# Windowed attention and FFN on one core: scores of a head pair on 64 rows each, values on 64 columns each, from float16 products

## The chip, the core and the metric

The kernel runs on one core of a Trainium2 chip. The core has a matrix engine (TensorE, PE in the profile; its weight loads are PEld), a vector engine (VectorE, DVE), an activation engine (ScalarE, ACT), a general engine (GpSimd, POOL) and a queue engine (SyncE, SP) that here issues DMA transfers. Each engine works through its own instructions in order; semaphores tie them together. The metric is device time in microseconds (us) of one execution, the median of several.

## The reference

Attention over 8 sequences of 576 positions with 8 heads of 64, each query seeing its own and the 127 positions before, with a bias that falls with distance (a slope of 2^-(head + 1)). Its output, 4608 rows of 512, goes through a feed-forward layer of width 2048.

```python
scores = scale * np.matmul(q, k.transpose(0, 1, 3, 2))
mask = (rel >= 0) & (rel < window)
scores = np.where(mask, scores + bias[None], -1000000000.0)
attn = np.exp(scores - np.max(scores, axis=-1, keepdims=True))
attn = attn / (np.sum(attn, axis=-1, keepdims=True) + 1e-09)
x = np.matmul(attn, v)
h = x @ w_in
g = np.where(h >= 1, h, np.where(h <= -1, 0.0, (h + 1) ** 2 / 4))
return g @ w_out
```

All of it is float32. The kernel keeps float32 accuracy with cheaper products: an operand is split into a high part and the rest, and products of the parts are summed.

## The kernel before

The 4608 rows are 12 chunks of 384 (three query blocks of 128). Per chunk, attention works through 4 head pairs (p, 48 in all), two heads m = 2p, 2p + 1 each; the FFN follows in 16 blocks of 128 columns (fc). Layer 1 of a block (L508 to L510) is 12 float16 matmuls of 384 columns, layer 2 (L539 to L541) 9 of 512, two blocks behind. While the FFN of chunk c runs, the attention of chunk c + 1 is emitted between its steps. Chunks 0 and 1 (LIGHT = 2) take plain float32 products in attention; chunk 0 also converts the float64 weights.

From chunk 2 on, a pair goes through these steps:

- q and k are loaded with both heads one above the other: 64 rows of head 0, 64 of head 1. `prepare_q` and `prepare_k` round them to a shorter float (qp, kp) and keep the rest, on ScalarE and VectorE. DMAs then copy the parts into ql (per head: q rounded on its 64 rows, q's rest on the other 64) and kk, kl (k rounded and k's rest, each on both halves): 12 copies per pair on SP's queue. With them two matmuls per block cover all products of the parts on 128 rows (L404, L405).
- `scores` takes one head: three blocks, two of them in a first PSUM bank, one in a second. VectorE adds the bias and takes the row minimum of the negated scores (L408), ScalarE takes the exponential with its sum (L410), VectorE normalises into ep (L416 to L421).
- `weights_t` transposes ep (L429), ScalarE and VectorE split it into float16 parts lu (L441, L442), GpSimd masks them (L444, L446).
- v is loaded (`load_v`, L294), its largest value found (`reach_of_v`, L302, VectorE), turned into a scale for the whole chunk (`scale_x`), and split into float16 parts vs (`prepare_v`, L373, L374).
- `values` takes one head: 8 matmuls (6 where no earlier block exists) whose 128 output rows hold the product with v's high part on 64 and with its rest on the other 64 (L483). ScalarE copies one half (L485), VectorE adds the other (L486) into xn.
- At the FFN's first step of a chunk, `split_x` makes the float16 parts xh and xl of xn (L501, L502), which layer 1 reads.

The order is written as a list, `segments`, one short function per entry, and a chunk's FFN step emits its share of the next chunk's entries. A scheduler then orders each engine's instructions by its own estimate of when each could start. Buffers that matter: the attention's PSUM pool has 3 banks, layer 1 has 2, vn has 6 tiles, z and ep 1, lu 2.

## Time and profile before

| | us |
|---|---|
| median of 3 runs (1077.75 to 1080.46) | 1077.77 |
| the profiled execution | 1081.46 |
| its span, first to last instruction | 1079.8 |
| TensorE busy in it | 995.4 (92%) |
| VectorE busy | 779.5 (72%) |
| ScalarE busy | 623.5 (58%) |
| GpSimd busy | 383.0 (35%) |

The mean granted TensorE clock of the profiled execution is 0.954 of full speed. A record of a matmul ends later than the next one starts, since matmuls are pipelined: a rate is read from starts. Row groups give the line in the program, the engine, the operation, output and inputs by name, the shape, the count, then busy time and the mean of one in ns, then the idle time of the engine just before them with what ended it.

### The profile page before, as it was taken

What the parts mean: (1) busy time and instruction counts of PE and PEld (TensorE: products, weight loads), DVE (VectorE), ACT (ScalarE), POOL (GpSimd) and SP (SyncE); (2) the same over time, 40 slices, a digit from 0 to 9 for tenths busy, and PEclk for the clock granted to TensorE, in tenths of its full rate; (3) what the DMA queues carried; (4) which work ended last, traced back from release to release, by engine and by line L of the source; (5) the groups of instructions that cost most, each with busy time, mean ns of one, the idle gap of its engine ahead of it and who ended that gap; (6) DMA issues with size and microseconds to landing.
All of it is one profiled execution on the core that took longest, in us unless ns stands there. A gap on an engine that the chain in (4) does not pass through costs nothing.

```text
span 1079.8 us, 17781 instructions
## 1 busy us (share of the span) xinstructions
PE 995.4 (92%) x5682; PEld 601.5 (56%) x5682; DVE 779.5 (72%) x2115; ACT 623.5 (58%) x1467; POOL 383.0 (35%) x461
## 2 busy tenths in 40 slices
...
GB/s 231 111 149 217 176 81 113 81 102 100 112 77 141 121 80 130 130 86 100 99 108 75 155 119 80 117 127 82 117 96 106 120 73 109 133 71 54 30 1 30
DMA packets 91677, 114.42 MB, mean 106 GB/s; under 512 B 11200, under 2 KB 66496, under 8 KB 91584
## 3 DMA queue, kind: packets, MB, share of 16 engines
...
q8 instruction: 45, 0.74, 0.3%
q14 instruction: 48, 0.39, 0.1%
...
## 4 chain that ended last, share of the span: by engine, by line
PE 47%; DVE 23%; DMA 12%; ACT 7%; SPq 5%; issue 4%; POOL 1%; ACTq 0%; DVEq 0%; POOLq 0%
PE h L508 7%; PE h L509 7%; PE h L510 7%; PE acc L539 6%; PE acc L540 6%; PE acc L541 6%; DMA vn<-in_v_dram 4%; ACT z L410 4%; DMA qr<-in_q_dram 4%; DVE g L516 3%; DMA ql<-qr 3%; DVE g L517 3%; DVE z L408 2%; SPq L364 2%; PE x L483 2%
## 5 line engine op out<-in xcount | busy, mean ns | idle before, releaser
L525 POOL TENSOR_TENSOR gl<-g,gh 128x384 f16<-128x384 f32 x176 | 170.0, 967 | 410.5 <-ACT gh L524 399.3
L508 PE MATMUL h<-xh,wi 128*128 128x384 f16 x768 | 255.7, 335 | 14.8 <-DVE g L517 12.5
L509 PE MATMUL h<-xl,wi 128*128 128x384 f16 x768 | 258.0, 336 | 11.8 <-DVE xl L502 11.7
L510 PE MATMUL h<-xh,wi 128*128 128x384 f16 x768 | 257.7, 336 | 0.5 <-DVE i_in L158 0.5
L516 DVE SCALAR_TENSOR_TENSOR g<-u,half 128x384 f32<-128x384 f32 x176 | 120.7, 688 | 116.1 <-ACT u L515 110.5
L539 PE MATMUL acc<-wo,gh 128*128 128x512 f16 x528 | 201.1, 381 | 0.0
L540 PE MATMUL acc<-wo,gh 128*128 128x512 f16 x528 | 200.8, 380 | 0.0
L541 PE MATMUL acc<-wo,gl 128*128 128x512 f16 x528 | 198.2, 379 | 0.0
L524 ACT CAST gh<-g 128x384 f16<-128x384 f32 x176 | 89.2, 510 | 179.1 <-DVE g L517 152.7
L410 ACT ACTIVATE z<-z,nmax 128x256 f32<-128x256 f32 (+2 forms) x288 | 138.5, 482 | 69.9 <-DVE nmax L408 67.0
L515 ACT ACTIVATE u<-h,shift,fall 128x384 f32<-128x384 f32 x176 | 116.5, 665 | 64.2 <-PE h L510 63.3
L444 POOL TENSOR_SCALAR_AFFINE_SELECT lu<-lu 128x768 f16<-128x768 f16 x80 | 74.1, 926 | 127.8 <-DVE lu L442 116.7
L509 PEld LDWEIGHTS <-wi 128*128 128x128 f16 x768 | 76.8, 100 | 72.9 <-issue 21.3
L510 PEld LDWEIGHTS <-wi 128*128 128x128 f16 x768 | 76.9, 100 | 66.5 <-issue 20.6
L517 DVE SCALAR_TENSOR_TENSOR g<-h,gain,g 128x384 f32<-128x384 f32 x176 | 107.5, 614 | 3.8
L508 PEld LDWEIGHTS <-wi 128*128 128x128 f16 x768 | 76.8, 100 | 58.3 <-issue 7.1
L408 DVE CUSTOM_DVE_ANT_0 z<-s,rel 128x256 f32<-128x256 f32 (+2 forms) x256 | 93.9, 392 | 6.5 <-PE s L405 3.2
L404 PE MATMUL s<-kk,ql 128*128 128x256 f32 (+2 forms) x240 | 77.8, 347 | 4.8 <-DVE xn L486 4.8
L541 PEld LDWEIGHTS <-gl 128*128 128x128 f16 x528 | 51.5, 98 | 54.8
L446 POOL TENSOR_SCALAR_AFFINE_SELECT lu<-lu 128x768 f16<-128x768 f16 x80 | 79.2, 989 | 4.9
L483 PE MATMUL x<-lu,vs 128*128 128x256 f16 (+1 forms) x592 | 68.1, 260 | 12.4 <-POOL lu L446 9.9
L539 PEld LDWEIGHTS <-gh 128*128 128x128 f16 x528 | 52.0, 98 | 48.8 <-issue 1.4
...
## 6 DMA issues: line engine op xcount, KB each, us to landing
...
```

The source lines that it names most:

```text
L408: V.tensor_tensor_reduce(out=z[:, i, c0:], in0=o, in1=r[:, c0:], op0=ALU.add, op1=ALU.min, scale=-slope if c else -0.125, scalar=3.0e38, a ...
L410: S.activation(z[:, i, c0:], z[:, i, c0:], AF.Exp, bias=nmax[:, i:i + 1], scale=-1.0, accum_out=sm[:, i, 0:1])
L508: T.matmul(ph, wi[fc][:, 0, cc, :], xh, start=(cc == 0), stop=False)
L509: T.matmul(ph, wi[fc][:, 0, cc, :], xl, start=False, stop=False)
L510: T.matmul(ph, wi[fc][:, 1, cc, :], xh, start=False, stop=(cc == NCC - 1))
L515: first = S.activation(u, ph, AF.Relu, bias=shift[c] if c else quarter, scale=fall[c][:, col])
L516: V.scalar_tensor_tensor(g, u, half[c] if c else 0.5, u, ALU.min, ALU.mult)
L517: last = V.scalar_tensor_tensor(g, ph, gain[c][:, col] if c else fall[c][:, col], g, ALU.mult, ALU.max)
L525: G.tensor_tensor(gl, g, gh, ALU.subtract)
L539: T.matmul(a, gh[:, ts], wo[fc][:, 0], start=first, stop=False)
L540: T.matmul(a, gh[:, ts], wo[fc][:, 1], start=False, stop=False)
L541: T.matmul(a, gl[:, ts], wo[fc][:, 0], start=False, stop=last)
```

## The change

From chunk 2 on:

- q and k stay on their own rows, head 0 on rows 0 to 63 and head 1 on 64 to 127, and are split into float16 parts there (`split_qk`), scaled by the largest values of q per row and of k for the chunk. Those come from ScalarE (`reach_of`, absolute value into a scratch tile with an accumulated result), VectorE and one matmul of 256 columns (`level`, `scale_all`). The bias tables and slopes are rescaled per chunk.
- `scores_of_pair` computes both heads at once: per block three products (high x high, high x rest, rest x high) for each head, each on 64 rows of the array, the two heads alternating, each head with a PSUM bank of its own.
- `values_of_pair` computes both heads into one bank: each product on 64 columns of the array, heads alternating. xh and xl are taken from that bank directly; copy, sum and `split_x` go.
- the DMA copies of q and k go; `load_all` requests q, k and v of a pair five pairs ahead.
- z and ep get two tiles, lu three. The list of segments is rewritten, so that a chunk counts as ready with its last pair's values.

```diff
         st = pair.setdefault(p, {})
         qr = st["qr"] = ap1.tile([P, CH], F32, name=f"qr_{p}", tag="qr")
         DMA.dma_start(qr, q[g * P:(g + 1) * P, c * CH:(c + 1) * CH])
+        kr = st["kr"] = kz[p % 2]
+        for j, r in enumerate(lo_rows):
+            DMA.dma_start(kr[r, j, :n], k[g * P + j * D:g * P + (j + 1) * D, (c + 1) * CH - n:(c + 1) * CH])
...
+    def load_all(p):
+
+        c, g = divmod(p, NPAIR)
+        n = CH + before(c) * P
+        if c == LIGHT:
...
+        pair[p] = dict(q=t[:, :CH], k=t[:, CH:CH + n])
+        DMA.dma_start(pair[p]["q"], q[g * P:(g + 1) * P, c * CH:(c + 1) * CH])
+        DMA.dma_start(pair[p]["k"], k[g * P:(g + 1) * P, (c + 1) * CH - n:(c + 1) * CH])
+        load_v(p)
...
+    def reach_of(p):
+
+        reach_of_v(p)
+        for x in "qk":
+            f = pair[p][x]
+            S.activation(junk[:, :f.shape[1]], f, AF.Abs, accum_out=tops[c, x][:, g:g + 1])
...
+    def level(c):
...
+        V.tensor_scalar(iq.bitcast(I32), rq.bitcast(I32), 0x7F800000, None, ALU.bitwise_and)
...
+        V.tensor_tensor(t, rk, iq, ALU.mult)
+        V.tensor_reduce(top[:, 0:1], t, X, ALU.max)
+        V.tensor_reduce(top[:, 1:2], tops.pop(c)[:, :NPAIR], X, ALU.max)
...
+        for a in range(2):
+            G.tensor_scalar(d[:, a], ident, top[:, a:a + 1], None, ALU.mult)
...
+    def scale_all(c):
...
+        T.matmul(b, ones, diag.pop(c).rearrange("p a w -> p (a w)"), start=True, stop=True)
...
+        V.tensor_reduce(i_2[c], b.rearrange("p (a w) -> p a w", w=P), X, ALU.max)
...
+        V.tensor_scalar(s_k[c], tops.pop((c, "i")), s_2[c][:, 0:1], None, ALU.mult)
+        V.tensor_scalar(z_of[c], fade, i_2[c][:, 0:1], None, ALU.mult)
...
+        V.tensor_scalar(rels[c][0], rel, s_2[c][:, 0:1], -1.0e38, ALU.mult, ALU.max)
...
+    def split_qk(p):
...
+        t = pair[p]["h"] = ap1.tile([P, 2, 2 * CH + P], F16, name=f"h_{p}", tag=("kl", "kk")[p % 2])
+        for x, s1, a, b in (("q", s_q[c], 0, CH), ("k", s_k[c], CH, CH + n)):
+            f, s1 = pair[p].pop(x), s1[:, g:g + 1]
+            S.activation(t[:, 0, a:b], f, AF.Copy, scale=s1)
+            V.scalar_tensor_tensor(t[:, 1, a:b], f, s1, t[:, 0, a:b], ALU.mult, ALU.subtract)
...
-        qp = ap1.tile([P, CH], F32R, name=f"qp_{p}", tag="qp")
-        S.activation(qp, qr, AF.Copy, scale=scale)
-        V.scalar_tensor_tensor(qr.bitcast(F32R), qr, scale, qp.bitcast(F32), ALU.mult, ALU.subtract)
...
-        for j in range(2):
-            DMA.dma_start(ql[lo_rows[j], j].bitcast(F32), qp[lo_rows[j]].bitcast(F32))
-            DMA.dma_start(ql[hi_rows[j], j].bitcast(F32), qr[lo_rows[j]])
-
-    def prepare_k(p):
...
-        S.copy(kp[:, :n], kr[:, :n])
-        V.tensor_tensor(kr[:, :n].bitcast(F32R), kr[:, :n], kp[:, :n].bitcast(F32), ALU.subtract)
...
-        for t, f in ((kk, kp.bitcast(F32)), (kl, kr)):
-            for j in range(2):
-                for r in lo_rows:
-                    DMA.dma_start(t[r, j, :n].bitcast(F32), f[lo_rows[j], :n])
...
-        S.activation(vs[:, :n, :, 0, :], vn[:, :n], AF.Copy, scale=s_x[c])
-        V.scalar_tensor_tensor(vs[:, :n, :, 1, :].rearrange("p i j d -> p (i j) d"), vn[:, :n].rearrange("p i j d -> p (i j) d"),
...
+        f = pair[p].pop("vn")[:, :n].rearrange("p i j d -> p i (j d)")
+        vs = pair[p]["vs"] = wp.tile([P, 2, NQB + 1, P], F16, name=f"vs_{p}", tag="f_i", bufs=3)
+        S.activation(vs[:, 0, :n], f, AF.Copy, scale=s_x[c])
+        V.scalar_tensor_tensor(vs[:, 1, :n], f, s_x[c], vs[:, 0, :n], ALU.mult, ALU.subtract)
...
+    def scores_of_pair(p, blks):
...
+        pts = [bank(f"s_{2 * p + j}_{blks[0]}").rearrange("r (m w) -> r m w", w=2 * P) for j in range(2)]
+        last = []
+        for n, i in enumerate(blks):
+            c0, k0 = window(c, i)
+            for s, (a, b) in enumerate(((0, 0), (0, 1), (1, 0))):
+                for j, r in ((1, lo_rows[1]), (0, lo_rows[0])):
+                    behind(last, lambda: last.append(
+                        T.matmul(pts[j][:, n, c0:], t[r, a, i * P:(i + 1) * P], t[r, b, CH + k0:CH + k0 + 2 * P - c0],
+                                 start=(s == 0), stop=(s == 2)).ins))
+                    last = last[-1:]
+        for j in range(2):
+            soften(2 * p + j, blks, pts[j])
+
...
+            head[m] = dict(ep=ap1.tile([P, NQB, P], F32, name=f"ep_{m}", tag="ep", bufs=2),
...
+                           ap1.tile([P, NQB, 2 * P], F32, name=f"z_{m}", tag="z", bufs=2),
...
-            T.matmul(o, ql[:, j, i * P:(i + 1) * P], kk[:, j, k0:k0 + 2 * P - c0], start=True, stop=False)
-            T.matmul(o, ql[:, j, i * P:(i + 1) * P], kl[:, j, k0:k0 + 2 * P - c0], start=False, stop=True)
...
+            factor = -0.125 if c == 0 else -2.0 ** -(m % H + 1) if c < LIGHT else z_of[c][:, m % H:m % H + 1]
+            V.tensor_tensor_reduce(out=z[:, i, c0:], in0=pt[:, n, c0:], in1=r[:, c0:], op0=ALU.add, op1=ALU.min,
+                                   scale=factor, scalar=3.0e38, accum_out=nmax[:, i:i + 1])
...
+        lu = head[m]["lu"] = ap1.tile([P, 2, 2 * NQB, P], F16, name=f"lu_{m}", tag="lu", bufs=3)
...
-        todo = [(i, s) for i in [*range(NQB), -1] if i + b0 >= 0 for s in range(2)]
-        for n, (i, s) in enumerate(todo):
-            w = vs[:, i + b0, j].rearrange("p s d -> p (s d)")
...
-            T.matmul(px[:, q0 * P:q1 * P], w, lu[:, s, first:first + q1 - q0, :].rearrange("p a w -> p (a w)"),
-                     start=(n == 0), stop=(n == len(todo) - 1), skip_group_check=True)
-        S.copy(o, px[D:, :])
-        V.tensor_tensor(o, px[:D, :], o, ALU.add)
...
+    def values_of_pair(p):
...
+        vs = pair.pop(p)["vs"]
+        lus = [head.pop(2 * p + j)["lu"] for j in range(2)]
+        px = bank(f"x_{p}")[:, :CH]
+        todo = [(i, a, b) for i in [*range(NQB), -1] if i + b0 >= 0 for a, b in ((0, 0), (0, 1), (1, 0))]
+        last = []
+        for n, (i, a, b) in enumerate(todo):
+            q0, q1 = max(i, 0), min(i + 2, NQB)
+            first = 2 * i + 1 if i >= 0 else 0
+            for j, r in enumerate(lo_rows):
+                behind(last, lambda: last.append(
+                    T.matmul(px[r, q0 * P:q1 * P], vs[:, a, i + b0, r], lus[j][:, b, first:first + q1 - q0, :].rearrange("p a w -> p (a w)"),
+                             start=(n == 0), stop=(n == len(todo) - 1), skip_group_check=True).ins))
+                last = last[-1:]
...
+        S.activation(xh, px, AF.Copy, scale=1.0 / TOP)
+        V.scalar_tensor_tensor(xl, px, 1.0 / TOP, xh, ALU.mult, ALU.subtract)
+        xs.setdefault(c, []).append((xh, xl))
...
+    for p in range(M1 // 2, NP):
+        c, g = divmod(p, NPAIR)
...
+        if new:
+            segments.append([lambda p=p: reach_of(p + NPAIR)])
+        segments.append([lambda p=p: scores_of_pair(p, (0, 1))])
+        if new and g == NPAIR - 1:
+            segments.append([lambda c=c: level(c + 1)])
+        segments.append([lambda p=p: scores_of_pair(p, (2,))])
+        segments.append([lambda p=p: split_v(p)])
+        if p > M1 // 2:
+            segments.append([lambda p=p: values_of_pair(p - 1)])
+            if g == 0:
+                ready.append(len(segments))
+        if new and g == NPAIR - 1:
+            segments.append([lambda c=c: scale_all(c + 1)])
+        segments.append([lambda p=p: weights_t(2 * p)])
+        segments.append(([lambda p=p: split_qk(p + 1)] if p + 1 < NP else []) + ([lambda p=p: load_all(p + 5)] if p + 5 < NP else []))
+        segments.append([lambda p=p: weights_t(2 * p + 1)])
+    segments.append([lambda: values_of_pair(NP - 1)])
+    ready.append(len(segments))
```

How it moves instructions, at three places. On VectorE, the boundary between the FFNs of chunks 8 and 9, before: attention's last sum of chunk 9 (xn_9_3, L486) and the split that layer 1 of chunk 9 waits for (xl_9_3, L502) stand behind the maximum of a v tile (rows_11) and next to work of chunk 10; block 15 of chunk 8 lies 27 rows ahead of the first of these.

```order
L302 TENSOR_REDUCE rows_11_9907<-vn_46_10188 128x1
L486 TENSOR_TENSOR xn_9_3_9788<-x_79_9909,xn_9_3_9788 64x384
L374 SCALAR_TENSOR_TENSOR vs_41_10185<-vn_41_8899,s_x10_9870,vs_41_10185 128x8x64
L408 ISA z_81_9976,nmax_81_9977<-s_81_0_9978,rel_110 128x256
L408 ISA nmax_81_9977 128x1
L408 ISA z_81_9976,nmax_81_9977<-s_81_0_9978,rel_end_122 128x256
L408 ISA nmax_81_9977 128x1
L408 ISA z_81_9976,nmax_81_9977<-s_81_2_9996,rel_110 128x192
L408 ISA nmax_81_9977 128x1
L329 TENSOR_SCALAR o_g10_10981<-r10_10978 128x1
L502 SCALAR_TENSOR_TENSOR xl_9_3_10033<-xn_9_3_9788,xh_9_3_10032 128x384
```

The same place after the change: xl_9_3 stands ahead of block 15 of chunk 8 (g_8_15, L593 and L594 now), and eight small rows lie between that block and g_9_0.

```order
L567 SCALAR_TENSOR_TENSOR xl_9_3_9863<-x_39_9843,xh_9_3_9862 128x384
L485 RECIPROCAL rc_80_9805<-rc_80_9805 128x3
L425 SCALAR_TENSOR_TENSOR vs_42_10318<-vn_42_9187,s_210_9628,vs_42_10318 128x512
L485 RECIPROCAL rc_81_9813<-rc_81_9813 128x3
L593 SCALAR_TENSOR_TENSOR g_8_15_9898<-u_8_15_9897,half8_8923 128x384
L489 TENSOR_TENSOR ep_80_9771<-z_80_9772,rc_80_9805 128x384
L408 TENSOR_SCALAR shift10_10910<-u10_10906 128x1
L326 TENSOR_SCALAR i_q11_10523<-rows_q11_9731 128x4
L489 TENSOR_TENSOR ep_81_9778<-z_81_9779,rc_81_9813 128x384
L594 SCALAR_TENSOR_TENSOR g_8_15_9898<-h_8_15_9884,gain8_8921,g_8_15_9898 128x384
```

What moved: the split that layer 1 needs went from the end of the boundary's work to ahead of it, and the next chunk's first scores went out of it.

On TensorE, the scores of one head before (chunk 6, emitted in chunk 5's FFN): six matmuls on the full array, with no weight-load rows of their own in the order.

```order
L510 MATMUL h_5_3_6164<-xh_5_3_5978,wi3_893 128x384
L404 MATMUL s_50_0_6069<-kk_25_5956,ql_25_6007 128x128
L405 MATMUL s_50_0_6069<-kl_25_5957,ql_25_6007 128x128
L404 MATMUL s_50_0_6069<-kk_25_5956,ql_25_6007 128x256
L405 MATMUL s_50_0_6069<-kl_25_5957,ql_25_6007 128x256
L404 MATMUL s_50_2_6096<-kk_25_5956,ql_25_6007 128x256
L405 MATMUL s_50_2_6096<-kl_25_5957,ql_25_6007 128x256
```

After, the end of a pair's scores and the start of the values of the pair before (L453 on 64 rows, heads 44 and 45 in turn; L557 on 64 columns, with the attention weights lu of heads 42 and 43):

```order
L453 MATMUL s_44_2_5288<-h_22_5176 128x256
L453 LDWEIGHTS h_22_5176
L453 MATMUL s_45_2_5289<-h_22_5176 128x256
L453 LDWEIGHTS h_22_5176
L453 MATMUL s_44_2_5288<-h_22_5176 128x256
L557 LDWEIGHTS vs_21_5079
L557 MATMUL x_21_5344<-lu_42_5149,vs_21_5079 64x256
L557 LDWEIGHTS vs_21_5079
L557 MATMUL x_21_5344<-lu_43_5199,vs_21_5079 64x256
```

What moved: a pair's scores are now 18 matmuls in three runs between FFN matmuls (one alone, 12, 5, mostly) and its values 24 (18) in one run behind the last of them, so that the array's form changes about seven times per pair.

More of the change, by code (lines that the diff above doesn't have):

```diff
@@ L103, in windowed_attention_then_ffn @@
         G.memset(qscale[D:, g:g + 1], 4.0 ** g / 2.0)
+    fade = const.tile([P, H], F32, name="fade")
+    for m in range(H):
+        G.memset(fade[:, m:m + 1], -2.0 ** -(m + 1))
     rel = const.tile([P, 2 * P], F32, name="rel")
@@ new lines, in scale_all @@
+    def scale_all(c):
+        b = bank(f"m_{c}")[:, :2 * P]
+        T.matmul(b, ones, diag.pop(c).rearrange("p a w -> p (a w)"), start=True, stop=True)
+        i_2[c], s_2[c] = column(f"i_2{c}", "i_2", 3, 2), column(f"s_2{c}", "s_2", 3, 2)
+        i_x[c], s_x[c] = i_2[c][:, 1:2], s_2[c][:, 1:2]
+        fall[c] = column(f"fall{c}", "fall", 2, NFC)
+        z_of[c] = column(f"z_of{c}", "z_of", 2, H)
+        V.tensor_reduce(i_2[c], b.rearrange("p (a w) -> p a w", w=P), X, ALU.max)
+        ti = i_2[c].bitcast(I32)
+        V.tensor_scalar(ti, ti, 0x7F800000, None, ALU.bitwise_and)
+        V.tensor_scalar(i_2[c], i_2[c], 2.0 ** -60, 1.0 / TOP, ALU.max, ALU.mult)
+        V.reciprocal(s_2[c], i_2[c])
+        V.tensor_scalar(s_k[c], tops.pop((c, "i")), s_2[c][:, 0:1], None, ALU.mult)
+        V.tensor_scalar(z_of[c], fade, i_2[c][:, 0:1], None, ALU.mult)
+        if "t" not in rels:
+            rels["t"] = rawp.tile([P, NQB, 2 * P], F32, name="rels", tag="rawo2")
+        rels[c] = rels["t"][:, c % 2], rels["t"][:, 2]
+        V.tensor_scalar(rels[c][0], rel, s_2[c][:, 0:1], -1.0e38, ALU.mult, ALU.max)
+        if c % CYCLE == 1:
+            V.tensor_scalar(rels[c][1], rel_end, s_2[c][:, 0:1], -1.0e38, ALU.mult, ALU.max)
@@ L366, in prepare_v @@
-    def prepare_v(p):
-        if p // NPAIR < LIGHT:
-            return
-        c = p // NPAIR
-        n = NQB + before(c)
-        vn = pair[p]["vn"]
-        vs = pair[p]["vs"] = ap1.tile([P, NQB + 1, 2, 2, D], F16, name=f"vs_{p}", tag="vs", bufs=2)
-        S.activation(vs[:, :n, :, 0, :], vn[:, :n], AF.Copy, scale=s_x[c])
-        V.scalar_tensor_tensor(vs[:, :n, :, 1, :].rearrange("p i j d -> p (i j) d"), vn[:, :n].rearrange("p i j d -> p (i j) d"),
-                               s_x[c], vs[:, :n, :, 0, :].rearrange("p i j d -> p (i j) d"), ALU.mult, ALU.subtract)
+            S.activation(ql, pair[p]["qr"], AF.Copy, scale=qscale[:, p % NPAIR:p % NPAIR + 1])
@@ new lines, in split_v, with window @@
+    def split_v(p):
+        c, g = divmod(p, NPAIR)
+        n = NQB + before(c)
+        f = pair[p].pop("vn")[:, :n].rearrange("p i j d -> p i (j d)")
+        vs = pair[p]["vs"] = wp.tile([P, 2, NQB + 1, P], F16, name=f"vs_{p}", tag="f_i", bufs=3)
+        S.activation(vs[:, 0, :n], f, AF.Copy, scale=s_x[c])
+        V.scalar_tensor_tensor(vs[:, 1, :n], f, s_x[c], vs[:, 0, :n], ALU.mult, ALU.subtract)
+    def window(c, i):
+        lone = i + before(c) == 0
+        c0 = P if lone else D if c % CYCLE == 1 and i == 2 else 0
+        return c0, (i + before(c) - 1) * P + c0
@@ L452, in values @@
         c, g = divmod(p, NPAIR)
-        vn, vs, lu = pair[p]["vn"], pair[p].get("vs"), head[m]["lu"]
+        vn, lu = pair[p]["vn"], head[m]["lu"]
         b0 = before(c)
@@ L499, in split_x @@
             xl = xp1.tile([P, CH], F16, name=f"xl_{c}_{cc}", tag=f"xl{cc}")
-            k = s_x[c] if c < LIGHT else 1.0 / TOP
-            S.activation(xh, xf, AF.Copy, scale=k)
-            V.scalar_tensor_tensor(xl, xf, k, xh, ALU.mult, ALU.subtract)
+            S.activation(xh, xf, AF.Copy, scale=s_x[c])
+            V.scalar_tensor_tensor(xl, xf, s_x[c], xh, ALU.mult, ALU.subtract)
             xs[c].append((xh, xl))
@@ L517, in layer1 @@
         last = V.scalar_tensor_tensor(g, ph, gain[c][:, col] if c else fall[c][:, col], g, ALU.mult, ALU.max)
+        done_g[fc if c == 0 else (c, fc)] = [first.ins, last.ins]
         if c == 0:
-            done_g[fc] = [first.ins, last.ins]
             gs[c, fc] = g
```

175 lines of the change are left out of this document (90 added, 85 removed).

## The prediction

> **What bounds the kernel now.** I read the table of stretches first. Columns: stretch in us, its length, busy time of each engine with its instructions, the granted TensorE clock, the DMA share and GB/s.
>
> ```profile
> 100.00:180.00 80.00, 72.22 (x341) 42.98 (x340) 75.93 (x236) 61.95 (x130) 20.98 (x26) 1.00 0.50 147
> 180.00:200.00 20.00, 12.97 (x61) 6.94 (x61) 17.16 (x36) 12.43 (x30) 5.39 (x6) 0.74 0.26 77
> 200.00:260.00 60.00, 59.86 (x370) 36.25 (x368) 41.18 (x111) 32.83 (x78) 20.60 (x22) 1.00 0.37 90
> ...
> 260.00:1000.00 740.00, 701.66 (x4150) 421.10 (x4149) 544.60 (x1434) 424.73 (x1016) 282.85 (x317) 0.96 0.43 105
> ```
>
> From 100 to 180 us (chunk 0) VectorE is full, 75.9 of 80. From 260 to 1000, nine chunks, TensorE is: 701.7 of 740 busy, nothing else over 74%. The same view of TensorE alone shows what it loses there.
>
> ```profile
> 360.00:420.00 60.00, 60.00 (x373) 1.00 0.44 103
> 780.00:840.00 60.00, 60.00 (x364) 1.00 0.40 95
> ...
> 760.00:780.00 20.00, 16.26 (x87) 0.83 0.49 132
> 780.00:800.00 20.00, 20.00 (x122) 1.00 0.39 93
> 800.00:820.00 20.00, 20.00 (x123) 1.00 0.40 96
> 820.00:840.00 20.00, 20.00 (x123) 1.00 0.42 96
> 840.00:860.00 20.00, 14.88 (x72) 0.74 0.60 162
> ```
>
> Undisturbed stretches have no idle time, clock 1.00 and 364 to 373 matmuls in 60 us, 6.14 per us. At that rate the 4150 matmuls of 260 to 1000 would take 676 us, so 64 us are lost: 38 (740 - 701.7) idle, the other 26 because the granted clock falls behind every idle gap (0.83 and 0.74 above). It happens once per chunk, where one chunk's FFN ends and the next begins. The timeline of the one at 842 us, VectorE, then TensorE (start, length, instruction, and in brackets the idle time ahead and who ended it):
>
> ```profile
> 841.87 0.23 DVE L328 TENSOR_SCALAR gain<-fall,half 128x16 f32<-128x16 f32 x1
> 843.37 0.69 DVE L302 TENSOR_REDUCE rows<-vn 128x1 f32<-128x512 f32 x1 [1.26 <-DMA vn<-in_v_dram]
> 844.09 0.55 DVE L486 TENSOR_TENSOR xn<-x,xn 64x384 f32<-64x384 f32 x1
> 844.67 0.75 DVE L374 SCALAR_TENSOR_TENSOR vs<-vn,s_x,vs 128x512 f16<-128x512 f32 x1
> ...
> 844.69 0.53 PE L404 MATMUL s<-kk,ql 128*128 128x192 f32 x1 [2.62 <-DVE xn L486]
> 845.24 0.85 PE L508 MATMUL h<-xh,wi 128*128 128x384 f16 x2
> 847.03 0.48 PE L509 MATMUL h<-xl,wi 128*128 128x384 f16 x1 [0.94 <-DVE xl L502]
> ```
>
> VectorE waits 1.26 us for a v tile that was requested just before, behind it stands the sum xn (L486) of the chunk's last head, behind that its split xl (L502), and layer 1 cannot pass without it. The next chunk's softmax, scale and split work stands there too: in VectorE's order 42 to 47 instructions lie between the g (L516) of the last FFN block of one chunk and that of the first block of the next, at each of the eight boundaries into chunks 3 to 10, against 23 into chunk 2, where the loss is small, as the window from 260 (18.08 of 20 busy, below) shows.
>
> ```profile
> 260.00:280.00 20.00, 18.08 (x98) 10.12 (x97) 15.09 (x43) 12.47 (x31) 9.04 (x10) 0.91 0.50 132
> ```
>
> That one is 1.9 idle and about as much in clock (0.09 x 20 = 1.8): 4 us. So the eight cost 64 - 4 = **60 us**, 7.5 each.
>
> **Term 1, boundaries.** After the change the last values of a chunk give xh and xl directly, without copy, sum and separate split; v is requested five pairs ahead without the q and k copies in SP's queue; and the piece of VectorE's order in the section on the change shows xl ahead of the last block. Counted in the same way, the rows into chunks 2 to 10 become 77, 29, 39, 12, 15, 14, 13, 14, 22. I price them by the rows above: 22 or 29 rows like the 23-row boundary (4 us), 39 like the others (7), 12 to 15 at 0.5, since the layer-1 matmuls no longer wait for anything in that piece. Into chunks 3 to 10: 4 + 7 + 5 x 0.5 + 4 = 17.5 instead of 60, a gain of 42. The bounds are 0 (each stall returns in another form) and 60. The work that left the boundary lies inside the chunk now, in one piece of some 20 rows between blocks 11 and 12, worth about 7 us; TensorE can run ahead over one layer-1 block (12 x 0.163) and two layer-2 blocks (18 x 0.216), 5.8 us (slots below). I charge 0.5 us per chunk, +4.
>
> The boundary into chunk 1 (44 rows to 16) improves, the one into chunk 2 (23 to 77) worsens. By group means VectorE's work ahead of chunk 2 is the same before and after, and chunk 0 is bound by it, so I take 0 for everything up to 260 us. The bounds are -10 (all of 180 to 200 that is lost: 7 idle, 0.26 x 20 = 5 of clock, less 2) and +10 (a piece of 77 rows against a chunk that had 19 us of VectorE idle from 200 to 260).
>
> **Term 2, TensorE's own work.** Ends of matmuls are modelled, so I use starts.
>
> ```profile
> 626.20 0.33 PE L510 MATMUL h<-xh,wi 128*128 128x384 f16 x1
> 626.23 0.41 PE L404 MATMUL s<-kk,ql 128*128 128x256 f32 x1
> 626.48 0.28 PE L405 MATMUL s<-kl,ql 128*128 128x256 f32 x1
> 626.60 0.28 PE L404 MATMUL s<-kk,ql 128*128 128x256 f32 x1
> 626.72 0.28 PE L405 MATMUL s<-kl,ql 128*128 128x256 f32 x1
> 626.84 0.34 PE L508 MATMUL h<-xh,wi 128*128 128x384 f16 x1
> ...
> 621.80 0.33 PE L510 MATMUL h<-xh,wi 128*128 128x384 f16 x1
> 621.96 0.38 PE L539 MATMUL acc<-wo,gh 128*128 128x512 f16 x1
> 622.18 0.38 PE L540 MATMUL acc<-wo,gh 128*128 128x512 f16 x1
> 622.40 0.82 PE L483 MATMUL x<-lu,vs 128*128 128x256 f16 x8
> 623.06 0.50 PE L429 MATMUL p<-ident,ep 128*128 128x128 f32 x3
> ```
>
> A 384-column float16 matmul holds its slot 0.16 us, one of 512 0.216 (0.42 ns a column). Four score matmuls fill 626.36 to 626.84: 0.12 each, 6 per head, 1.44 per pair. The eight value matmuls (1536 columns) fill 622.40 to 623.06: 0.66 per head, 0.11 for 256 columns and 0.055 for 128. Chunks 3, 6 and 9 have no block before, 0.55 per head. Over 40 pairs: 28 x (1.44 + 1.32) + 12 x (1.44 + 1.10) = 108 us.
>
> After: 18 score matmuls per pair on 64 rows, 24 value matmuls on 64 columns (18 in 12 pairs), heads alternating. If the two heads' halves of the array run side by side, a couple takes one slot: 9 x 0.11 = 0.98 for scores, 6 x 0.11 + 6 x 0.055 = 0.98 or 0.82 for values, 28 x 1.96 + 12 x 1.80 = 76.5, a gain of **31**. If they take turns it is 153, a loss of 45. No row shows two matmuls at once; I take side by side, since the operands' rows, the output columns and the PSUM banks are disjoint, and keep the other as a rival. The Trainium skill (TensorE: Matmul & The Clock Gate, Measured speedup vs the span model) gives 3.07 for four row tiles and 2.38 for three column tiles, some 78% of ideal. By that, as an estimate, this would be 98 us, 21 more than in my sum; no run here shows it yet.
>
> Against it stands the change of form. In the new order TensorE goes 295 times from the full array to half rows, to half columns or back, about 7 times per pair. Rows show only switches between float32 and float16, and these cost nothing visible: four scores take 0.48 between two float16 matmuls, six 0.72. The bounds are 0, and a full drain: the 0.38 - 0.216 = 0.16 us that a matmul's record lasts beyond its slot, plus one weight load.
>
> ```profile
> L509 PEld LDWEIGHTS <-wi 128*128 128x128 f16 x768 | 76.8, 100 | 72.9 <-issue 21.3
> ```
>
> That load is 0.10, so 0.26 each, 78 us in all. I take the load alone, 0.10, as if weights could not be fetched ahead across a switch: **+30**. The rule that speaks against the change is in the Trainium skill (TensorEngine Tiling (Array Packing), Key Properties): another tiling mode drains the TensorE, another tile does not. It gives no time; by it the price is above 0, without it my sum would be 30 lower.
>
> **Term 3, the other engines.**
>
> ```profile
> L485 ACT COPY xn<-x 64x384 f32<-64x384 f32 x80 | 38.0, 475 | 23.7 <-PE x L483 22.0
> L343 ACT ACTIVATE qp<-qr,qscale 128x384 fp32r<-128x384 f32 x40 | 24.6, 614 | 17.0 <-DMA qr<-in_q_dram 15.1 <-issue 1.6
> L356 ACT CAST kp<-kr 128x512 fp32r<-128x512 f32 x28 | 17.3, 618 | 36.2 <-DMA kr<-in_k_dram 34.9 <-issue 0.7 <-DMA kk<-kp 0.4
> L373 ACT ACTIVATE vs<-vn,s_x 128x512 f16<-128x512 f32 x28 | 20.0, 718 | 0.5
> L214 ACT ACTIVATE junk<-wf 128x512 bf16<-128x512 f32 x16 | 10.0, 628 | 3.5 <-DVE top_i L157 2.4 <-DVE top_x L157 0.5 <-DVE wf L175 0.4
> L214 ACT ACTIVATION_READ_ACCUMULATOR junk<-wf 128x1 f32 x16 | 3.1, 191 | 0.0
> L486 DVE TENSOR_TENSOR xn<-x,xn 64x384 f32<-64x384 f32 x80 | 43.7, 547 | 15.7 <-ACT xn L485 14.3
> L344 DVE SCALAR_TENSOR_TENSOR qr<-qr,qscale,qp 128x384 fp32r<-128x384 f32 x40 | 26.6, 666 | 7.9 <-ACT qp L343 7.7
> L357 DVE TENSOR_TENSOR kr<-kr,kp 128x512 fp32r<-128x512 f32 x28 | 22.2, 792 | 30.5 <-ACT kp L356 17.7 <-DMA qr<-in_q_dram 11.6 <-DMA vn<-in_v_dram 1.2
> ```
>
> ScalarE loses the 80 copies (38) and the roundings of q and k (25 and, with the 12 narrower ones, 23); it gains 80 splits like L373, 0.6 to 0.7 each (52), and 80 maxima like L214 with a readout of 0.19 (60): +26 us. VectorE loses 44 + 27 + 30 and gains 53 for the splits (0.6 to 0.75 each) and about 3 per chunk for scales: some -18. GpSimd gains ten matrices of about 0.9. All of it lies under TensorE's 75 us per chunk (4150 / 9 / 6.14) and costs nothing, as long as no piece outlasts TensorE's lead (charged above); uncovered, +26 is the price. The DMA copies of q and k leave SP's queue; they mattered through the late v above.
>
> **Sum.** 1081.5 (profiled run, 1.7 beyond its span of 1079.8) - 42 + 4 - 31 + 30 = 1042. The median of the runs is 3.7 below the profiled one: **1038**.
>
> **Rivals.**
> - *Cheap switches.* The float32 to float16 rows speak for it. At 0.02 each the 30 becomes 6: 1014; with all boundaries gone, 996.
> - *Halves take turns*, the change not doing what it says. For: no record of two matmuls at once. Price +76: 1114, slower. It decides once a couple of 256 columns takes 0.17 instead of 0.11 us (40 us over 76.5).
> - *Full drain*, 0.26 each: +48, 1086, slightly slower.
> - *New waits for banks.* The scores pool has 3 banks; a pair's first step takes two at once, and its third block needs one back from VectorE (4 reductions of 0.5 us). For: VectorE was late before. Against: some 23 FFN matmuls (4 us) lie between the steps. At 0.75 us a pair: +30, 1068.
>
> **Chances.** Forecast (1018 to 1056) 0.50; cheap switches 0.20; bank waits 0.12; turns 0.10; full drain 0.08. No change means within 0.3%, 3 us, about what a measurement of this kernel can tell. Faster: 0.50 + 0.20 + 0.09 of the bank waits = 0.79; same 0.05 (the rest of the bank waits, a quarter of the drains); slower 0.16 (the turns, the other drains). The range leaves out the turns, the full drain and the best corner: 996 to 1080.
>
> **What would show it.** Stretches of 20 us at boundaries into chunks 5 to 10 with 20.00 busy and clock 1.00: term 1 right; still 15 busy and 0.8: wrong. Starts of an alternating couple within 0.03 us, and 0.11 to the next couple: side by side; 0.11 apart: turns. The gap between the last full-array matmul and the first half-row one, less 0.216, is the switch; 0.2 or more sinks the forecast. Waits of TensorE's scores on VectorE's reduction (L408, L476 then) inside a chunk would be the banks. Wrong also if the stretch from 180 to 260 takes over 10 us longer.

## The result, and the profile after

The changed kernel takes 1030.89 us (median of 4 runs, 1026.92 to 1032.61), the kernel before 1077.98 beside it: a ratio of 0.9553 with a 95% interval of 0.9522 to 0.9584, 47 us faster. The forecast was 1038 (996 to 1080). The profiled execution took 1030.51 us, its span is 1028.3, 51.5 us shorter than before.

The page of the changed kernel: busy times with shares and instructions by engine, and the shares of the chain of work that ended last.

```profile
PE 975.1 (95%) x6218; PEld 548.8 (53%) x6218; DVE 742.2 (72%) x2128; ACT 618.2 (60%) x1547; POOL 374.7 (36%) x479
...
PE 81%; DVE 8%; DMA 4%; ACT 3%; issue 2%; POOL 1%; ACTq 0%; SPq 0%; DVEq 0%; POOLq 0%
```

The shares of the chain before:

```profile
PE 47%; DVE 23%; DMA 12%; ACT 7%; SPq 5%; issue 4%; POOL 1%; ACTq 0%; DVEq 0%; POOLq 0%
```

TensorE's share of the chain rises from 47% to 81%, VectorE's falls from 23% to 8%. Where TensorE still loses time stands in the table of stretches (busy time with instructions, granted clock, DMA share, GB/s), TensorE alone:

```profile
180.00:200.00 20.00, 19.98 (x115) 1.00 0.01 2
...
240.00:260.00 20.00, 13.19 (x109) 0.86 0.35 113
260.00:280.00 20.00, 15.59 (x99) 0.72 0.12 36
...
340.00:360.00 20.00, 17.10 (x94) 0.91 0.21 73
...
420.00:440.00 20.00, 16.43 (x129) 0.91 0.22 73
440.00:1020.00 580.00, 580.00 (x3865) 1.00 0.11 34
```

From 440 to 1020 us no idle time shows and the granted clock is 1.00, seven boundaries between chunks (into 5 to 11) included. What is left, as idle time plus (1 - clock) x 20: 9.6 and 10.0 us at 240 to 280 (chunk 2 begins at 238.6), 4.7 at 340 (chunk 3 begins at 336.9), 5.4 at 420 (chunk 4 begins at 416.3). A chunk "begins" here with the start of its first layer-1 matmul. What TensorE waited for there (total, times, longest), the longest waits at 230 to 285, at 335 to 365 and at 415 to 445 us:

```profile
PE s L453 <- DVE nmax L476: 3.4, 1, 3.4
PE h L585 <- ACT x L566: 3.1, 1, 3.1
...
PE h L585 <- DVE g L594: 2.9, 1, 2.9
...
PE s L453 <- DVE lu L510: 3.6, 1, 3.6
```

The scores (L453) read neither nmax nor lu. In the kernel these two VectorE rows are the last to read a PSUM bank of the attention's pool of three, so both are waits for a bank.

One of the free boundaries, that into chunk 9, on VectorE (start, length, instruction, idle time ahead):

```profile
802.38 0.62 DVE L594 SCALAR_TENSOR_TENSOR g<-h,gain,g 128x384 f32<-128x384 f32 x1
...
804.15 0.85 DVE L368 SCALAR_TENSOR_TENSOR h<-qk,s_q,h 128x384 f16<-128x384 f32 x1 [0.48 <-ACT h L367]
...
806.66 0.54 DVE L567 SCALAR_TENSOR_TENSOR xl<-x,xh 128x384 f16<-128x384 f32 x1
...
807.93 0.58 DVE L593 SCALAR_TENSOR_TENSOR g<-u,half 128x384 f32<-128x384 f32 x1
```

and on TensorE:

```profile
805.11 0.38 PE L618 MATMUL acc<-wo,gl 128*128 128x512 f16 x1
805.32 0.33 PE L585 MATMUL h<-xh,wi 128*128 128x384 f16 x1
...
806.62 0.33 PE L587 MATMUL h<-xh,wi 128*128 128x384 f16 x1
806.79 0.38 PE L616 MATMUL acc<-wo,gh 128*128 128x512 f16 x1
807.00 0.33 PE L585 MATMUL h<-xh,wi 128*128 128x384 f16 x1
```

The split xl (L567) of the chunk's last pair ends at 807.2, 1.9 us after layer 1 of chunk 9 has begun (805.32). TensorE works on the parts of x that are there, then on layer 2 of the chunk before, and no row shows idle time.

### The profile page after: what moved, and what is told of

Its sections match the earlier page's. It is cut to its first block, busy times and chain, and to the rows that moved or that the text cites. A ratio compares the mean times of both kernels' runs of the same rounds, so it can differ in the third digit from the quotient of the medians.

```text
span 1028.3 us, 17951 instructions
## 1 busy us (share of the span) xinstructions
PE 975.1 (95%) x6218; PEld 548.8 (53%) x6218; DVE 742.2 (72%) x2128; ACT 618.2 (60%) x1547; POOL 374.7 (36%) x479
## 4 chain that ended last, share of the span: by engine, by line
PE 81%; DVE 8%; DMA 4%; ACT 3%; issue 2%; POOL 1%; ACTq 0%; SPq 0%; DVEq 0%; POOLq 0%
PE h L585 11%; PE h L587 11%; PE h L586 11%; PE acc L616 11%; PE acc L617 11%; PE acc L618 11%; PE s L453 5%; PE x L557 4%; PE p L497 3%; DMA vn<-in_v_dram 2%; PE acc L613 2%; PE x L536 1%; DVE g L593 1%; ACT z L478 1%; DVE g L594 1%
## 5 line engine op out<-in xcount | busy, mean ns | idle before, releaser
L602 POOL TENSOR_TENSOR gl<-g,gh 128x384 f16<-128x384 f32 x176 | 164.8, 936 | 394.1 <-ACT gh L601 375.9
L593 DVE SCALAR_TENSOR_TENSOR g<-u,half 128x384 f32<-128x384 f32 x176 | 121.0, 689 | 178.1 <-ACT u L592 167.9
L585 PE MATMUL h<-xh,wi 128*128 128x384 f16 x448 | 146.4, 328 | 3.7 <-DVE g L594 3.7
L587 PE MATMUL h<-xh,wi 128*128 128x384 f16 x448 | 147.4, 329 | 1.3 <-DVE wi L214 1.3
L586 PE MATMUL h<-xl,wi 128*128 128x384 f16 x448 | 147.2, 328 | 0.0
L476 DVE CUSTOM_DVE_ANT_0 z<-s,rels,z_of 128x256 f32<-128x256 f32 (+2 forms) x240 | 98.4, 459 | 26.8 <-PE s L453 26.4
L594 DVE SCALAR_TENSOR_TENSOR g<-h,gain,g 128x384 f32<-128x384 f32 x176 | 107.8, 614 | 3.8
L585 PE MATMUL h<-x,wi 128*128 128x384 f16 x320 | 105.3, 331 | 4.4 <-ACT x L566 3.1
L586 PEld LDWEIGHTS <-wi 128*128 128x128 f16 x768 | 75.7, 99 | 62.2 <-issue 9.2
L585 PEld LDWEIGHTS <-wi 128*128 128x128 f16 x768 | 75.5, 98 | 62.1 <-issue 6.6
L586 PE MATMUL h<-x,wi 128*128 128x384 f16 x320 | 105.9, 331 | 0.2 <-DVE x L567 0.2
L587 PE MATMUL h<-x,wi 128*128 128x384 f16 x320 | 105.9, 331 | 0.0
L587 PEld LDWEIGHTS <-wi 128*128 128x128 f16 x768 | 75.7, 99 | 54.6 <-issue 4.2
L512 POOL TENSOR_SCALAR_AFFINE_SELECT lu<-lu 128x768 f16<-128x768 f16 x80 | 72.5, 914 | 71.0 <-DVE lu L510 56.7
L618 PEld LDWEIGHTS <-gl 128*128 128x128 f16 x528 | 51.5, 98 | 58.6 <-issue 1.1
```

Of the source, the lines that this page charges most:

```text
L476: V.tensor_tensor_reduce(out=z[:, i, c0:], in0=pt[:, n, c0:], in1=r[:, c0:], op0=ALU.add, op1=ALU.min, scale=factor, scalar=3.0e38, accum_ ...
L585: T.matmul(ph, wi[fc][:, 0, cc, :], xh, start=(cc == 0), stop=False)
L586: T.matmul(ph, wi[fc][:, 0, cc, :], xl, start=False, stop=False)
L587: T.matmul(ph, wi[fc][:, 1, cc, :], xh, start=False, stop=(cc == NCC - 1))
L593: V.scalar_tensor_tensor(g, u, half[c] if c else 0.5, u, ALU.min, ALU.mult)
L594: last = V.scalar_tensor_tensor(g, ph, gain[c][:, col] if c else fall[c][:, col], g, ALU.mult, ALU.max)
```

## The experiments

Each ran beside the kernel before on the same chip, whose median was 1076.86 to 1078.55 us throughout, so medians are compared with the 1030.89 of the changed kernel. "Form" is full array, half rows (scores) or half columns (values); a "couple" is one matmul of each head, next to each other.

**1. The price of a change of form.** Three extra matmuls of 64 columns per pair are put between the couples of the scores' first block, into a part of the bank that is written later; once on 128 rows, once on 64.

```diff
                     last = last[-1:]
+                if len(blks) > 1 and n == 0:
+                    behind(last, lambda: last.append(
+                        T.matmul(pts[0][:, 1, P:P + D], t[:, 0, :P], t[:, 0, CH + P:CH + P + D], start=False, stop=True, skip_group_check=True).ins))
+                    last = last[-1:]
```

In the second kernel the operands are `t[lo_rows[0], 0, :P]` and `t[lo_rows[0], 0, CH + P:CH + P + D]`.

> The changed kernel with three extra matmuls of 64 columns per pair of heads, on the full array (128 rows), each between two couples of the scores' first block: 120 matmuls, 236 more switches of form. At 0.10 us a switch: 24 us + 120 x 0.027 = +27 us over the changed kernel. If a switch is cheap (0.02): +8. If it is a full drain (0.26): +65.

> The same 120 extra matmuls of 64 columns at the same places, but on 64 rows, in the form of their neighbours: no switch of form is added. Every theory: +3 us (0 to +6); the difference to the run on the full array is the price of 236 switches.

Measured: 1054.81 us (ratio 0.9801, 0.9769 to 0.9833) on the full array, 1032.35 (0.9583, 0.9552 to 0.9614) on half rows. The difference of 22.5 us over 238 changes of form (531 against 293 in the traces) is **0.094 us each**; the forecast took 0.10. The timeline of the first, TensorE:

```profile
534.00 0.23 PE L453 MATMUL s<-h 64*128 64x128 f16 x1
534.15 0.20 PE L458 MATMUL s<-h 128*128 128x64 f16 x1
534.29 0.23 PE L453 MATMUL s<-h 64*128 64x128 f16 x2
534.45 0.20 PE L458 MATMUL s<-h 128*128 128x64 f16 x1
534.59 0.23 PE L453 MATMUL s<-h 64*128 64x128 f16 x2
```

From one extra matmul to the next it is 0.30 us: a couple of 128 columns (0.055), the 64 columns (0.027), and two changes, 0.11 each.

**2. Both heads on the same rows.** The scores of both heads are taken from rows 0 to 63.

```diff
-                for j, r in ((1, lo_rows[1]), (0, lo_rows[0])):
+                for j, r in ((1, lo_rows[0]), (0, lo_rows[0])):
```

> The changed kernel, but the scores of both heads are taken from rows 0 to 63 (those of head 0 twice), so that the two matmuls of a couple need the same half of the array; order, switches and everything else are the same. If couples of the scores run side by side in the changed kernel: 9 x 0.109 us more per pair, 40 pairs, +39 us (30 to 42), the starts of a couple 0.109 apart. If they take turns anyway: 0 to +3.

Measured: 1059.97 us (0.9835, 0.979 to 0.9879), +29 us, a little under the 30 to 42. The same run of twelve score matmuls in the changed kernel, then in this one (each with the full-array matmul behind it):

```profile
527.58 0.72 PE L453 MATMUL s<-h 64*128 64x128 f16 x12
528.24 0.39 PE L617 MATMUL acc<-wo,gh 128*128 128x512 f16 x1
```

```profile
538.91 1.21 PE L453 MATMUL s<-h 64*128 64x128 f16 x12
540.05 0.39 PE L617 MATMUL acc<-wo,gh 128*128 128x512 f16 x1
```

0.66 us against 1.14. Couples do run side by side on the two halves, and without that the changed kernel gives back most of its gain. The 39 us were a little too many: a pair's 18 score matmuls run as twelve, one alone and five. Twelve take 12 turns instead of 6 (1.508 instead of 0.857 us for 3072 columns), five take 5 instead of 3 (1.855 instead of 1.637 with 24 value matmuls behind them), the lone one loses nothing: 0.87 us a pair, less where blocks are narrower, about 32 us in all.

**3. Heads one after the other.** The loops over heads and products change places.

```diff
-            for s, (a, b) in enumerate(((0, 0), (0, 1), (1, 0))):
-                for j, r in ((1, lo_rows[1]), (0, lo_rows[0])):
+            for j, r in ((1, lo_rows[1]), (0, lo_rows[0])):
+                for s, (a, b) in enumerate(((0, 0), (0, 1), (1, 0))):
...
-        for n, (i, a, b) in enumerate(todo):
+        for j, r in enumerate(lo_rows):
+            for n, (i, a, b) in enumerate(todo):
...
-            for j, r in enumerate(lo_rows):
```

> The changed kernel, but each head's products stand together (three per block for the scores, all of a pair for the values) instead of alternating, so that neighbouring matmuls use the same half of the array. If the alternating couples run side by side and that is what makes the change affordable: 9 x 0.109 us more per pair for the scores (39 us), 0.98 or 0.82 for the values (37 us), 46 more switches of form at 0.10 (5 us), so +80 us over the changed kernel, some 1110, slower than the kernel before. If couples take turns anyway and the gain is all from the boundaries: within 6 us of the changed kernel (switches only). If packing is worth 78% of ideal: about +55.

Measured: 1062.48 us (0.9867, 0.9835 to 0.99), +32, a miss by all three. The reason is in the starts. In the program a run of twelve scores is now three of head 1, three of head 0, three of head 1, three of the next; the records start, in us after the first:

```
scores, 12 of 256 columns:  0  0.010  0.120  0.130  0.229  0.239  0.338  0.348  0.447  0.457  0.556  0.566
values, 24 of a pair, columns (start) from the seventh on:
128 (0.679) 128 (0.735) 128 (0.791) 256 (0.797) 128 (0.847) 128 (0.903) 256 (0.930) 128 (0.959) 256 (1.039)
```

The scores start in couples all the same: a matmul on the free half passes those that stand ahead of it for the other half. Twelve of 3072 columns took 0.864 us, against 0.857 alternating. In the values, whose order is twelve of one head (6 x 256, 6 x 128) and then twelve of the other, the tenth to start (at 0.797) has 256 columns. So it is the second head's first, and three of the first head's are still to come, in 26 of 26 such runs. So TensorE passes two or three matmuls, not twelve: a pair's values took 2.00 us (1.61 without a block before) where two changes of form and ideal halves make 1.18 (1.02), 30 us over all pairs. That is about the measured loss; the scores lost little but 46 more changes of form (4 us). In this kernel alternating was needed only where twelve stand in a row, not where three do.

**4. What holds the boundary: the place of VectorE's work.** Attention is emitted three steps later, nothing else. (All engines' attention work moves with it. The expectations count VectorE's rows from the last g row, L594, of one chunk to the first of the next; the prediction counted from L593 to L593, which gives 12 to 15 where they say 10 or 11.)

```diff
-            emit_attention(int(now + (end - now) * (r + (4 if c else 7)) / STEPS))
+            emit_attention(int(now + (end - now) * (r + (1 if c else 7)) / STEPS))
```

> The changed kernel with attention emitted three FFN steps later (a lead of 1 step instead of 4), all operations the same; VectorE's rows at the boundaries into chunks 5 to 10 become 28, 28, 39, 28, 27, 23 instead of 10 or 11 (17 into 10), the direct split stays. If the rows in that piece are the price of a boundary: 4 us for each with 23 to 28 and 7 with 39, +20 us over the changed kernel (15 to 28). If the split alone was: 0 to +5.

Measured: 1064.64 us (0.9881, 0.9852 to 0.9909), +34 where 15 to 28 were expected; its profiled execution, at the low end of its runs, has a span 28.4 us longer. TensorE in its stretches, and what it waited for from 500 to 975 us (total, times, longest):

```profile
590.00:600.00 10.00, 7.09 (x46) 1.00 0.31 111
...
670.00:680.00 10.00, 6.67 (x39) 0.83 0.33 111
...
750.00:760.00 10.00, 7.81 (x47) 0.87 0.46 151
```

```profile
PE s L453 <- DVE lu L510: 8.0, 3, 3.3
PE h L585 <- DVE g L594: 7.3, 3, 3.0
```

The stalls are back, with VectorE late for g, or for lu, whose row is the last reader of a bank that the scores need. How long each chunk takes from its beginning to the next one's, worked out from the starts of the first layer-1 matmuls:

| chunk | 5 | 6 | 7 | 8 | 9 | 10 |
|---|---|---|---|---|---|---|
| changed kernel, us | 75.7 | 76.4 | 76.8 | 75.9 | 76.6 | 75.3 |
| lead of 1 step, us | 80.0 | 80.1 | 82.6 | 79.4 | 80.7 | 77.4 |
| VectorE's rows at the boundary into it, lead of 1 | 28 | 28 | 39 | 28 | 27 | 23 |

The differences, 4.3, 3.7, 5.8, 3.5, 4.1 and 2.1, are 23.5 us and follow the rows: 4 for some 28, 6 for 39, 2 for 23. This is about the price that the prediction put on them, on the same operations; 1.7 of it are 18 more changes of form, the rest mostly idle time (15.3) and clock (5.1). Of the other 4.9 us of the profiled execution 1.0 lie ahead of chunk 5 and 4.0 in chunk 11, where TensorE stands 2.3 us for g. The some 6 us that the median lost beyond this execution are not explained.

**5. The late split.** Values go to a float32 tile first and are split at the chunk's first FFN step, into one set of tiles.

```diff
...
-        S.activation(xh, px, AF.Copy, scale=1.0 / TOP)
-        V.scalar_tensor_tensor(xl, px, 1.0 / TOP, xh, ALU.mult, ALU.subtract)
-        xs.setdefault(c, []).append((xh, xl))
+        xn[c, g] = xp1.tile([P, CH], F32, name=f"xn_{c}_{g}", tag=f"xn{g}")
+        S.copy(xn[c, g], px)
...
-            if fc == 0 and c < LIGHT:
+            if fc == 0:
```

> The changed kernel, but values are copied to float32 (ScalarE, 0.5 us per pair) and split into xh and xl at the chunk's first FFN step into one set of tiles, as before the change; VectorE rows at the boundaries stay at 10 or 11. If the direct split into its own tiles is what freed the boundaries: 2 to 5 us per boundary come back, +20 to +45 us over the changed kernel. If it is that the boundary holds 10 rows of VectorE's work instead of 45: +0 to +10.

Measured: 1036.08 us (0.9608, 0.9585 to 0.963), +5. In its stretches:

```profile
340.00:360.00 20.00, 18.93 (x132) 1.00 0.16 47
...
420.00:440.00 20.00, 19.57 (x135) 1.00 0.21 73
500.00:950.00 450.00, 448.22 (x3032) 1.00 0.11 36
```

From 500 to 950 us it idles 1.8 us in all, besides 20 more changes of form in the whole program (2 us): under 1 us per boundary where 2 to 5 were expected. The direct split is not what freed the boundaries. The run also moved rows that the expectation did not name: into chunks 3 and 4 its trace has 11 each instead of 28 and 39, and the stalls there are nearly gone (1.2 and 0.4 us idle in these chunks, against 2.9 and 3.6); into chunk 2 it has 84 instead of 78, and 240 to 280 us lose 25 instead of 19.6. So the +5 is a balance, and the price of rows shows a second time.

**6. One tile of z and ep, two of lu.**

```diff
-            head[m] = dict(ep=ap1.tile([P, NQB, P], F32, name=f"ep_{m}", tag="ep", bufs=2),
+            head[m] = dict(ep=ap1.tile([P, NQB, P], F32, name=f"ep_{m}", tag="ep"),
...
-                           ap1.tile([P, NQB, 2 * P], F32, name=f"z_{m}", tag="z", bufs=2),
+                           ap1.tile([P, NQB, 2 * P], F32, name=f"z_{m}", tag="z"),
...
-        lu = head[m]["lu"] = ap1.tile([P, 2, 2 * NQB, P], F16, name=f"lu_{m}", tag="lu", bufs=3)
+        lu = head[m]["lu"] = ap1.tile([P, 2, 2 * NQB, P], F16, name=f"lu_{m}", tag="lu", bufs=2)
```

> The changed kernel with one tile each of z and ep and two of lu, as before the change. VectorE's rows at the boundaries into chunks 3 to 10 become 19, 18, 18, 18, 19, 18, 17, 11 instead of 28, 39, 10, 10, 10, 11, 9, 17, and there are 62 more switches of form (6 us). If 18 rows cost 4 us each: 5 x 3.5 - 3 + 6, +20 us over the changed kernel. If some 18 rows are still hidden by what TensorE has queued: +6 or less.

Measured: 1040.88 us (0.9652, 0.9612 to 0.9692), +10: between the two.

```profile
500.00:950.00 450.00, 445.09 (x2988) 1.00 0.11 36
```

Idle time is 4.9 us where the changed kernel has none, so 18 rows cost about 1 us per boundary, not 4; the 62 changes of form are worth 6.

**7. The kernel before, with v earlier.** Two attempts: v on GpSimd's DMA queue, past the copies in SP's; and v requested a pair earlier.

```diff
-        DMA.dma_start(t[:, :nb].rearrange("p i j d -> p i (j d)"),
+        (G if c >= LIGHT else DMA).dma_start(t[:, :nb].rearrange("p i j d -> p i (j d)"),
```

```diff
-            loads = [p + 4] if p < NPAIR else [p + 4, p + 5] if p == NPAIR else [p + 5]
+            loads = [p + 4] if p < NPAIR else [p + 4, p + 5, p + 6] if p == NPAIR else [p + 6]
```

> The kernel before, with v requested on GpSimd's DMA queue from chunk 2 on, so that it no longer stands behind the copies of q and k in SP's queue. The VectorE rows at the boundaries stay at 43 to 49. If the late v was what made the boundaries stall: VectorE's waits for v (rows, L302) go and 20 to 50 us of the 60 go with them, 1030 to 1055. If v was only the last to come, and the 43 to 49 rows of other work ahead of the layer-1 input are the cost: within 10 us of the kernel before.

> The kernel before, with v requested one pair earlier (six ahead instead of five); the order of VectorE's rows is the same row by row (37 to 47 at the boundaries). If the late v stalls the boundaries: VectorE's waits for v (41.6 us) fall below 10 and the time by 15 to 40 us, to 1040 to 1063. If the 38 to 47 rows between the last block of a chunk and the first of the next are the cost: within 8 us of the kernel before.

Measured: 1096.60 us (1.0164, 1.0132 to 1.0195) and 1076.55 (0.9983, 0.9958 to 1.0007). Neither made v earlier, and the first is 18 us slower, outside both its expectations. VectorE's wait in the first, then in the second with what SP waited for:

```profile
DVE rows L302 <- DMA vn<-in_v_dram: 46.1, 32, 5.5
```

```profile
DVE rows L302 <- DMA vn<-in_v_dram: 42.6, 30, 3.7
...
SPq L294 <- DVE vs L374: 158.1, 21, 11.7
```

In the second, the request itself stands 158 us in SP's queue until a tile of v comes free (vs, L374), as it stood 155.8 us in the kernel before. In the first, GpSimd stands 41.7 us (16 times) before its requests, waiting for the same rows of VectorE, with its own work behind them. By these waits the six tiles set when v is asked for, not the place of the request; no run had more tiles. What an earlier v alone would do stays open.

**8. The kernel before, with the copies of k on ScalarE's queue.**

```diff
-                    DMA.dma_start(t[r, j, :n].bitcast(F32), f[lo_rows[j], :n])
+                    S.dma_start(t[r, j, :n].bitcast(F32), f[lo_rows[j], :n])
```

> The kernel before, with the eight DMA copies of k per pair on ScalarE's queue instead of SP's; all arithmetic is the same. By the scheduler's own estimate attention then ends earlier, and the rows at the boundaries into chunks 3 to 10 become 29, 18, 14, 15, 19, 18, 29, 25 instead of 38 to 47. If these rows are the cost: 4 us for each boundary of 18 to 29 and 0.5 for 14 and 15, 25 instead of 60, so 35 us faster than the kernel before, some 1043, though no product is cheaper. If the gain of the change lies in its own operations: within 8 us of the kernel before, or slower by what 320 more issues cost ScalarE.

Measured: 1128.78 us (1.0462, 1.0416 to 1.0508), 51 us slower, against both. ScalarE's waits:

```profile
ACT u L515 <- DMA kl<-kr: 70.6, 20, 5.5
...
ACT u L515 <- DMA kk<-kp: 21.8, 5, 4.8
ACT gh L524 <- DMA kl<-kr: 14.6, 4, 4.3
```

Its u and gh, which the FFN needs, now stand 107 us behind copies. The rows left the boundary (18, 14, 15, 19 and 18 into chunks 4 to 8 in its trace), and layer 1's waits for xl fell from 11.7 us to 2.3; but a new wait came with the move, so this run does not tell whether the rows were the whole cost in the kernel before.

**9. Two versions against the stalls left.** The maxima of the pair four ahead, and the scales, are emitted behind a pair's scores; then, in addition, q, k and v six pairs ahead.

```diff
-        if new:
-            segments.append([lambda p=p: reach_of(p + NPAIR)])
         segments.append([lambda p=p: scores_of_pair(p, (0, 1))])
-        if new and g == NPAIR - 1:
-            segments.append([lambda c=c: level(c + 1)])
         segments.append([lambda p=p: scores_of_pair(p, (2,))])
+        if new:
+            segments.append([lambda p=p: reach_of(p + NPAIR)])
+        if new and g == NPAIR - 1:
+            segments.append([lambda c=c: level(c + 1)])
...
-        segments.append(([lambda p=p: split_qk(p + 1)] if p + 1 < NP else []) + ([lambda p=p: load_all(p + 5)] if p + 5 < NP else []))
+        segments.append(([lambda p=p: split_qk(p + 1)] if p + 1 < NP else []) + ([lambda p=p: load_all(p + 6)] if p + 6 < NP else []))
```

> The changed kernel with the maxima of the pair four ahead (v on VectorE, q and k on ScalarE), and the scales made from them, emitted behind the scores of a pair instead of ahead of them. In the changed kernel they wait for loads requested one step before (VectorE 21.6 us for v tiles in all), and with a chunk's first blocks queued behind, TensorE stands still 2.9 us near 346 us. If stalls behind a late v are what is left of the boundary losses: 3 to 10 us faster than the changed kernel, and the stretch 340 to 360 us full. If they are hidden everywhere else: 0 to 4 us faster.

> The run with the maxima behind the scores, and every pair's q, k and v requested one pair earlier (six ahead). If the stalls left at 340 to 360 and 420 to 440 us come from v that lands after VectorE is there: VectorE's waits for v fall from 17.8 us to under 5, these two stretches are full, and the time is 4 to 12 us below that run. If they come from the work itself: 0 to 3 us below it.

Measured: 1024.78 us (0.952, 0.9491 to 0.9548) and 1028.06 (0.9524, 0.9489 to 0.9558), the lowest medians of all, though their intervals overlap that of the changed kernel; the second, expected below the first, is not. TensorE in the first:

```profile
240.00:260.00 20.00, 13.77 (x115) 0.96 0.34 113
260.00:280.00 20.00, 19.27 (x110) 0.79 0.17 50
340.00:360.00 20.00, 16.77 (x122) 1.00 0.21 70
```

and in the second:

```profile
240.00:260.00 20.00, 9.52 (x91) 0.74 0.37 118
260.00:280.00 20.00, 18.58 (x118) 0.91 0.21 67
340.00:360.00 20.00, 17.25 (x124) 1.00 0.21 70
```

What the first gains lies at 240 to 280 us: 12 lost instead of 19.6, with 52 rows of VectorE into chunk 2 instead of 78 (counted as in the expectations). The second has 78 again and loses 18.9 there. The stretch at 340 is full in neither, against both expectations, and VectorE's waits for v in the second are still 15.4 us (under 5 expected): the stalls left are not explained by late loads.

## Why the prediction held, and where it was off

The sum was 1042 against 1081.5 for the profiled run, -39.5; the span fell by 51.5. The measured column adds up to -48; some 4 us are not assigned.

| step | predicted | measured |
|---|---|---|
| boundaries into 3 to 10 | 60 to 17.5 | 60 to 10.1 (4.7 at 340, 5.4 at 420) |
| pieces inside the chunk | +4 | 0 |
| TensorE's own work | -31 + 30 | +2 |
| up to the boundary into 2 | 0 | -12 at 180 to 200, then +16 at 240 to 280 |
| boundary into 11 | not counted | -4 |

- **What bounds the kernel**: right. TensorE is full for 580 us on end, as the 20-us stretches were to show.
- **Term 1** was right in kind: experiment 4 gives the price per row back on the changed kernel's own operations. It was mis-sized in the small pieces: those of 12 to 22 rows (by the prediction's count) cost nothing (0.5 for each of five, 4 into 10 and 4 inside the chunks had been charged, 10.5 us), while 29 and 39 rows came out at 4.7 and 5.4 against 4 and 7. It also left out the boundary into chunk 11, where the kernel before lost 4 us (7.58 of 10 busy from 1010 us on, clock 0.83).
- One reason named in term 1 was wrong: the direct split is worth nothing at these boundaries (experiment 5). The second, v without the copies ahead of it, could not be tested (experiment 7). Shown is that the place of attention's work decides, to be read off VectorE's rows at the boundary, and that the second tiles are part of it (experiment 6). Which other part of the change lets attention end earlier stays open; no run emitted the attention of the kernel before earlier with its own operations.
- **Term 2**: right in both halves. Couples start 3 ns apart, and twelve scores of 3072 columns take 0.857 us less two changes of form, against 0.653 for ideal halves. By the prediction's estimate from the Trainium skill (TensorE: Matmul & The Clock Gate, Measured speedup vs the span model) it would have been 21 us more; the two halves here lose nothing in these runs. A pair's scores and values take 0.308 + 0.857 + 1.637 = 2.80 us against 2.76 before: halves and changes cancel. With the rule that another tiling mode drains the TensorE (the Trainium skill, TensorEngine Tiling (Array Packing), Key Properties) the trace agrees: a change costs 0.094 us.
- **Term 3**: right. ScalarE's splits of q and k take 50.6 us and its maxima 59.7 (52 and 60 predicted), and from 440 to 1020 us that costs TensorE nothing; at 240 to 280 TensorE waits 3.1 us for ScalarE's x. ScalarE's busy time falls all the same, from 623.5 to 618.2 us: the lengths of its instructions add up to 728 us against 707, but more of them overlap.
- **Up to 260 us** the sum of 0 hides two effects. The stall at 180 to 200 went, and with 77 rows into chunk 2 a larger one came at 240 to 280 (19.6 us against 4). That the two nearly cancel is luck.
- **Rivals**: cheap changes of form, a full drain and turns fell to experiments 1 and 2. New waits for banks, expected inside chunks, do not appear from 440 to 1020 us, where TensorE waits for nothing. At two boundaries they do: 3.4 us for nmax and 3.6 for lu, 7.0 of the 17.7 us idle in the four stretches above, and 8.0 of the 15.3 in experiment 4. VectorE's late rows stop TensorE there by way of a bank. Before, scores also waited 4.8 us (for xn, L486).
